# One transformer block on one NeuronCore: the down-projection's whole first pass by seven products, its sums turned back inside the second pass

## The chip, the cores and the metric

The kernel runs on one core of a Trainium2 chip. The metric is the device time of one execution in microseconds (us). The kernel before takes 1741.13 us, the median of three runs (1739.67 to 1741.83). The profiled execution, to which all rows of the trace belong, took 1740.01 us.

Five engines work in parallel, each on its own list of instructions in a fixed order: TensorE (PE in the profile, with its weight loads as PEld), VectorE (DVE), ScalarE (ACT), GpSimd (POOL) and SyncE (SP), which here issues nearly all DMA transfers. An instruction that waits for another engine holds up everything behind it on its own engine.

## The reference

One block works on 2048 tokens of width 512 in float32: attention and a gated feed-forward part, each behind a layer norm that is scaled and shifted by a conditioning vector.

```python
x = A_x                                        # (1, 2048, 512)
mod = (silu(c) @ w_mod).reshape(1, 6, 1, 512)  # sa, ca, ga, sb, cb, gb
h = layernorm(x) * (1 + ca) + sa
q = (h @ wq)                                   # 32 heads of 128; 8 heads of keys and values
p = softmax(q @ k.T * 128 ** -0.5)             # keys: the last 512 of the cache
x = x + ga * (p @ v) @ wo
h = layernorm(x) * (1 + cb) + sb
x = x + gb * ((gelu(h @ w_gate) * (h @ w_up)) @ w_down)   # 512 -> 1792 -> 512
```

## The kernel before

**Precision.** Every float32 operand of a product is split into a high half (float16) and a low half (what the high half leaves, again float16). A product is three matmuls, high by high, high by low and low by high, summed in PSUM (`mm3`, called at line 90 of the profile's numbering). The high halves are made by ScalarE as a copy, the low halves by a subtraction on VectorE or POOL. Weights are scaled so that they fit float16: the row norms are squared and summed on ScalarE (`sumsq`), summed across partitions by two-column matmuls (`sums`, tile `pst`) and turned into scales by small POOL and VectorE instructions (`f_spread`, `d_spread`).

**Seven products.** A product of two by two blocks is made of seven block products instead of eight (`PROD`, `CHAIN`, `ORDER`). This takes sums and differences of blocks beforehand (of weights on POOL during their preparation; of activations `t1` to `t4`) and adding up of the seven results.

**Stages.** Attention runs in 512 steps of about 2.6 us (`T` = 512), each with one score tile `ps`, its row maximum on VectorE, its exponential on ScalarE (line 993), its halves, a transpose by DMA (`pt<-p`, issued by SyncE) and the products with the values (`po`). The tokens go through in two halves of 1024. Projections of queries (`qa`, `qb`, `qc`) and of the attention's output (`py<-wo,ot`) fill TensorE between the score tiles. In the second half of attention the feed-forward weights are prepared beside this: loaded, scaled, combined on POOL, split, and stored to DRAM (`kept<-stage`). `prep_set` does so for the gate and up weights, `prep_wd` for the down weights. Their steps are planned by labels of attention steps (`sched`, `at`), and their buffers come from small pools: `raw` (five buffers, shared with the combination blocks `cb`, the staged products and later the rows `yr`), `rw` (two) and `wr` (two). A load is issued by SyncE when the buffer's earlier user has finished.

**Feed-forward part.** It starts at about 1345 us and has two passes of 1024 tokens. Each pass goes over seven pairs `n` of 128-wide tiles of the 1792 inner columns (`NP` = 7, so `n` = 0 to 13), and each pair has two projections `q = 2n + m`: gate (`m` = 0) and up (`m` = 1). Each projection is seven products of six matmuls in the order 1, 2, 6, 7, 5, 4, 3 (`ORDER`), in PSUM tiles `fa`, `fb`, `fc`. ScalarE copies the first, the second and the third chain's beginning out of PSUM (`keep`, line 887, tiles `fg`, `u`, `fu`), VectorE adds the rest (line 1272), and gate results go through GELU on ScalarE (line 1278); up results are multiplied with them on VectorE (line 1288), and the product is split (`high_of`, line 1298, and `low_of`, line 1302) for the down-projection.

**Down-projection.** In each pass the pairs up to the fifth (`turned(n)` true) use seven products. Their result comes transposed (columns of the model in partitions, tokens along the row), is scaled with a column per partition (`dyc`) and summed in float32 in SBUF over the pairs (`yt_add`, line 1678, tiles `yt`, VectorE). Sums of the activations' blocks for it are made on POOL (`sums_of`, line 1314). The last two pairs of each pass (`NROW` = 2) use plain row products (`y_tasks`, tile `py`), whose result has tokens in partitions and is added to the rows `acc` by VectorE (line 954). The plain weights carry the output's gain per column; the turned ones have it in `dyc`. So the transposed sums have to be turned back: ScalarE splits each float32 word into two 16-bit planes (`yt_turn`, line 1697, `yu<-yt`), a DMA transposes them (`yv<-yu`), POOL joins them again into rows (`yt_row`, line 1715, `yr<-yv`) and adds them to `acc` (`whole`, line 1657). In both passes this happens during the last two pairs: the chain ends with the fifth pair, and the sums turn while the row products run. The rows after attention (`y1`) are loaded to `acc` at the same place (`rows_in`).

**Order of the work.** The order on each engine is that in which the code issues it, with no planner behind it in this part. `tick` advances a counter after each product, and `put_off(d, f)` issues `f` that many products later. Products of the previous pair's down-projection are inserted between the products of the projection, after product index 1, 2, 5 and 6 (`y_next`), two at a time. Fetches of the next weights are issued at fixed product indices (`f_at(q, k, ...)`).

## Time and profile before

| what | value |
|---|---|
| median of three runs | 1741.13 us (1739.67 to 1741.83) |
| profiled execution | 1740.01 us |
| its span, first to last instruction | 1737.8 us |
| TensorE busy | 1712.5 us, 8020 matmuls |
| VectorE busy | 1426.1 us |
| ScalarE busy | 1242.4 us |
| POOL busy | 1056.9 us |
| moved by DMA | 339.82 MB, mean 196 GB/s |

How to read it: the page gives the busy time of each engine over the whole span, while the answers for a window (from:to in us from the start of the span) give it by stage. A row of the timeline has the start, the duration, the engine, the line of the kernel (L90 is line 90), the operation, the tile written and the tiles read, the shapes and a count of joined instructions; in brackets stands the time for which the engine had stood idle, and what ended it. A matmul's own duration is that of its passage through a pipeline: the next one starts before it ends, so the spacing of starts is what counts. A wait is put down to what came last. Rows of groups give busy time and mean duration in ns, then idle time before them.

### The profile page before, as it was taken

To read this page: it belongs to the slowest core of one execution; us is meant where nothing else is said; L and a number is where in the kernel's file an instruction comes from. 1 tells how busy PE (TensorE), PEld (TensorE's weight loads), DVE (VectorE), ACT (ScalarE), POOL (GpSimd) and SP (SyncE) were. 2 spreads that over 40 slices of the span, in tenths; PEclk is the share of its full clock that TensorE was granted. 3 is DMA by queue.
4 is the path that set the end of the run, shared out by engine and by line. 5 is a ranking of instruction groups with operands and counts; after the bars stand their busy time and mean duration, and the time that the engine had idled before them with its cause. 6 is when DMAs were issued, how large, how long until landed. Compare 5 with 4: busy or idle time off the path is not lost.

```text
span 1737.8 us, 26247 instructions
## 1 busy us (share of the span) xinstructions
PE 1712.5 (99%) x8020; PEld 786.6 (45%) x8022; DVE 1426.1 (82%) x2462; ACT 1242.4 (71%) x2797; POOL 1056.9 (61%) x1274
## 2 busy tenths in 40 slices
PE   7999999999999999999999999999999999999998
PEld 4444444444444444444444444444444444444444
DVE  7898898988888899888888888888986778666666
ACT  6988788888878777897778787777785455533442
POOL 4889778776788884654665665754720346733424
PEclk9999999999999999999999999999999999999999
DMA  7999999999999999999999999999996556633353
GB/s 233 222 202 213 216 212 208 222 203 221 219 216 233 201 209 187 213 209 229 199 221 223 207 230 210 198 229 214 199 189 151 158 160 207 167 121 119 95 157 103
DMA packets 690636, 339.82 MB, mean 196 GB/s; under 512 B 578880, under 2 KB 601408, under 8 KB 690496
## 3 DMA queue, kind: packets, MB, share of 16 engines
q1 hardware_dynamic: 690208, 337.63, 86.0%
q8 instruction: 63, 1.03, 0.3%
q14 instruction: 77, 0.63, 0.1%
q10 hardware_dynamic: 288, 0.52, 0.1%
HBM read 135.66 MB, written 61.87 MB: 114 GB/s over the span
## 4 chain that ended last, share of the span: by engine, by line
PE 86%; DVE 5%; ACT 4%; POOL 2%; DMA 2%; issue 1%; SPq 0%; DVEq 0%; POOLq 0%; ACTq 0%
PE py L90 20%; PE po L90 17%; PE ps L90 17%; PE qa L90 8%; PE fa L90 7%; PE qc L90 4%; PE fc L90 4%; PE ya L90 2%; PE qb L90 2%; PE fb L90 2%; DMA pt<-p 1%; PE yc L90 1%; ACT p L1005 1%; ACT ee L993 1%; PE pq L90 1%
## 5 line engine op out<-in xcount | busy, mean ns | idle before, releaser
L993 ACT ACTIVATE ee<-ps,nm 128x512 f32<-128x512 f32 x512 | 350.0, 684 | 191.9 <-DVE nm L984 189.8
L1010 DVE SCALAR_TENSOR_TENSOR p<-ee,rr,p 128x512 f16<-128x512 f32 x512 | 460.1, 899 | 4.7 <-ACT p L1005 4.3
L984 DVE TENSOR_REDUCE nm<-ps 128x1 f32<-128x512 f32 x512 | 350.1, 684 | 104.5 <-PE ps L90 101.1
L90 PE MATMUL ps<-k,qt 128*128 128x512 f16 x1536 | 414.9, 379 | 6.4 <-ACT ee L993 5.3
L1005 ACT ACTIVATE p<-ee,rr 128x512 f16<-128x512 f32 x512 | 364.5, 712 | 20.0 <-DVE rr L1001 10.1
L90 PE MATMUL po<-pt,v 128*128 128x512 f16 x1536 | 373.0, 379 | 2.0 <-DMA pt<-p 1.9
L90 PE MATMUL py<-wo,ot 128*128 128x512 f16 x1536 | 371.5, 379 | 0.0
L90 PEld LDWEIGHTS <-w 128*128 128x128 f16 x2184 | 213.3, 98 | 261.5 <-issue 4.2
L90 PEld LDWEIGHTS <-v 128*128 128x128 f16 x1536 | 149.8, 98 | 184.5 <-issue 2.4
L90 PEld LDWEIGHTS <-ot 128*128 128x128 f16 x1536 | 150.3, 98 | 181.6 <-DVE ot L742 0.5
L90 PEld LDWEIGHTS <-qt 128*128 128x128 f16 x1536 | 145.9, 98 | 177.7 <-issue 4.9
L1314 POOL TENSOR_TENSOR fg<-fg 128x512 f32<-128x512 f32 x40 | 52.8, 1319 | 153.9 <-DVE fg L1288 151.5
L742 DVE SCALAR_TENSOR_TENSOR ot<-po,ot 128x512 f16<-128x512 f32 x128 | 87.7, 685 | 39.3 <-ACT ot L741 38.9
L1298 ACT ACTIVATE at<-fg 128x512 f16<-128x512 f32 x86 | 53.9, 628 | 90.9 <-DVE fg L1288 75.4
L993 ACT ACTIVATION_READ_ACCUMULATOR ee<-ps,nm 128x1 f32 x512 | 99.9, 195 | 0.0
L954 DVE SCALAR_TENSOR_TENSOR acc<-py,ysc,acc 128x512 f32<-128x512 f32 x128 | 94.7, 739 | 5.3 <-PE py L90 5.3
L235 POOL TENSOR_TENSOR lw<-lw,half__86 128x1 f32<-128x1 f32 x37 | 23.4, 633 | 105.4 <-DVE lw L185 105.3
L90 PE MATMUL qa<-t,w 128*128 128x512 f16 x348 | 84.9, 379 | 0.0
L90 PE MATMUL fa<-t,w 128*128 128x512 f16 x336 | 81.6, 379 | 1.8 <-ACT fg L887 0.9
L397 POOL TENSOR_TENSOR rs<-rs,nhalf 128x1 f32<-128x1 f32 x32 | 18.8, 586 | 102.6 <-DVE rs L391 99.8
L741 ACT ACTIVATE ot<-po 128x512 f16<-128x512 f32 x128 | 73.8, 577 | 5.0 <-PE po L90 5.0
L159 POOL TENSOR_TENSOR stage<-rw,stage 128x512 f16<-128x512 f32 (+1 forms) x56 | 64.4, 1150 | 4.7
(241 smaller groups left out, 2761.5 us busy)
## 6 DMA issues: line engine op xcount, KB each, us to landing
w<-kept SPq DMA_DIRECT2D x123, 256.0 KB, 3.3
wo<-kept SPq DMA_DIRECT2D x70, 256.0 KB, 3.2
kept<-stage SPq DMA_DIRECT2D x61, 256.0 KB, 3.2
raw<-in_wo SPq DMA_DIRECT2D x56, 256.0 KB, 3.2
kept<-w SPq DMA_DIRECT2D x39, 256.0 KB, 3.2
rw<-in_wq SPq DMA_DIRECT2D x38, 256.0 KB, 3.2
hs<-hf SPq DMA_DIRECT2D x32, 256.0 KB, 2.8
pt<-p SPq DMA_TRANSPOSE x512, 3.5
```

The source lines that it names most:

```text
L90: nc.tensor.matmul(ps, a, b, start=first and n == 0, stop=last and n == 2, skip_group_check=chain)
L159: nc.gpsimd.tensor_tensor(dst[:, 1, :], src, dst[:, 0, :], op=ALU.subtract)
L235: nc.gpsimd.tensor_tensor(out, out, half_, op=ALU.pow)
L741: nc.scalar.activation(t[:, 0, :], src, AF.Copy, scale=scale)
L742: return lambda: nc.vector.scalar_tensor_tensor(t[:, 1, :], src, scale, t[:, 0, :], op0=ALU.mult, op1=ALU.subtract)
L954: nc.vector.scalar_tensor_tensor(acc[ti], st["p"], by, acc[ti], op0=ALU.mult, op1=ALU.add)
L984: nc.vector.tensor_reduce(nm, E[t]["ps"], axis=AX.X, op=ALU.max, negate=True)
L993: nc.scalar.activation(e, E[t]["ps"], AF.Exp, bias=E[t]["nm"], scale=1.0, accum_out=sm[:, t % 2:t % 2 + 1])
L1005: nc.scalar.activation(p16[:, 0, :], E[t]["e"], AF.Copy, scale=E[t]["r"])
L1010: nc.vector.scalar_tensor_tensor(p16[:, 1, :], E[t]["e"], E[t]["r"], p16[:, 0, :], op0=ALU.mult, op1=ALU.subtract)
L1298: nc.scalar.activation(t[:, 0, :], g, AF.Copy)
L1314: nc.gpsimd.tensor_tensor(g[o], g[a], g[b], op=ALU.subtract)
```

## The change

All seven pairs of the first pass now take the seven products in the down-projection (`turned(n)` is true for `n < NP`); in the second pass the last two pairs keep the row products. Since the two forms need differently prepared weights, the down weights of pairs 5 and 6 (counted from 0) are prepared twice: in turned form at the old place, stored under `wd`, and as plain rows at steps 455 and 490 of attention, stored under `wr` (`by_rows` gives their columns in `dsc` and `dysc`). The chain of the first pass thus ends with pair 6, whose products run during pair 7 of the second pass, and the sums of the first 1024 tokens are split, transposed and joined there. The joining copy `yr` of the first pass moves from POOL to ScalarE (`yt_row`); POOL then adds the row of `y1`, loaded into buffers of tag `h` (`rows_of_first`), to it, and the row goes out by DMA two products later (`first_out`). Splits and copies are put off by other numbers of products than before.

In the projections, the GELU of block 11 is put off by three products instead of two, the high half of block 11 of the very last up projection by two; the high halves of `t1`, `t2`, `t3`, `t4` are issued 2, 4, 4, 5 products later (before: 2, 4, 3, 5; for the first pair now 4, 5, 6, 6 and before 4, 6, 5, 6), and the low halves in the order `t2`, `t1`, `t3`, `t4` at 5, 5, 6, 6 (one more each for the first pair).

```diff
--- before.py
+++ after.py
@@ -172,7 +172,7 @@
 
     for name, n in (("kmax", HKV), ("kinv", HKV), ("vmax", HKV), ("vsc", HKV), ("wsc", HQ // 2), ("qsc", HQ // 2),
                     ("ksc", HQ // 2), ("osc", HKV), ("ysc", HKV), ("fsc", NF), ("finv", NF), ("gsc", NF // 2),
-                    ("dsc", NF // 2), ("dysc", NF // 2), ("dyc", KT * NF // 2), ("ma", 1), ("mf", 1), ("gam", 2)):
+                    ("dsc", NF // 2 + NROW), ("dysc", NF // 2 + NROW), ("dyc", KT * NF // 2), ("ma", 1), ("mf", 1), ("gam", 2)):
         stats(name, n)
 
     def col(name, i=0):
@@ -292,7 +292,11 @@
 
     def turned(n):
 
-        return n % NP < NP - NROW
+        return n < NP or n % NP < NP - NROW
+
+    def by_rows(n):
+
+        return NP + n % NP - (NP - NROW)
 
     def f_spread(i, m):
         w = little("lw", 1, 2)
@@ -304,18 +308,19 @@
             pool_ts(g, col("finv", i), 1.0 / GU)
             then(lambda: nc.vector.reciprocal(g, g))
 
-    def d_spread(n, m, more):
+    def d_spread(n, m, more, rows_):
         w, t = little("lw", 1, 2), little("lt", 1, 2)
         norm2(w, m, 2, 1.0)
-        pool_ts(w, w, 1.0 if turned(n) else col("gam", 1), 1.0 / TOP14)
+        d = by_rows(n) if rows_ else n
+        pool_ts(w, w, col("gam", 1) if rows_ else 1.0, 1.0 / TOP14)
         pool_ts(w, w, 1e-30, 1.0, ALU.max)
         pool_ts(t, col("finv", 2 * n), 2.0 ** 19, col("finv", 2 * n + 1))
-        pool_ts(col("dysc", n), t, 2.0 ** 19, w)
-        if turned(n):
+        pool_ts(col("dysc", d), t, 2.0 ** 19, w)
+        if not rows_:
             pool_ts(ST["dyc"][:, KT * n:KT * (n + 1)], cols[:, 5, :], col("dysc", n))
 
         def second():
-            nc.vector.reciprocal(col("dsc", n), w)
+            nc.vector.reciprocal(col("dsc", d), w)
             more()
 
         then(second)
@@ -1282,7 +1287,7 @@
 
         def result(key, src):
             if m == 0:
-                put_off(2 if key == "11" else 0, gelu(key, src)[0])
+                put_off(3 if key == "11" else 0, gelu(key, src)[0])
             else:
                 g = G[n, key]
                 nc.vector.scalar_tensor_tensor(g, g, col("gsc", n % NP), src, op0=ALU.mult, op1=ALU.mult)
@@ -1302,7 +1307,7 @@
             eng.tensor_tensor(t[:, 1, :], g, t[:, 0, :], op=ALU.subtract)
 
         def parts(key, g):
-            high_of(key, g)
+            put_off(2 if key == "11" and q == NQ - 1 else 0, lambda: high_of(key, g))
             if key in ("22", "21"):
                 st.setdefault("low", []).append(lambda: low_of(key, g, nc.vector))
             else:
@@ -1312,10 +1317,11 @@
             g = {k: G.pop((n, k)) for k in ("11", "12", "21", "22")}
             for o, a, b in (("11", "12", "11"), ("12", "22", "12"), ("22", "22", "11"), ("21", "21", "22")):
                 nc.gpsimd.tensor_tensor(g[o], g[a], g[b], op=ALU.subtract)
-            late = 0 if n else 2
-            for key, o, high, low in (("t1", "11", 2, 5), ("t3", "12", 3, 6), ("t2", "22", 4, 5), ("t4", "21", 5, 6)):
-                put_off(high + (late if high < 5 else late // 2), lambda key=key, o=o: high_of(key, g[o]))
-                put_off(low + late // 2, lambda key=key, o=o: low_of(key, g[o], nc.gpsimd))
+            src = {"t1": "11", "t2": "22", "t3": "12", "t4": "21"}
+            for key, high in zip(src, (2, 4, 4, 5) if n else (4, 5, 6, 6)):
+                put_off(high, lambda key=key: high_of(key, g[src[key]]))
+            for key, low in (("t2", 5), ("t1", 5), ("t3", 6), ("t4", 6)):
+                put_off(low + (not n), lambda key=key: low_of(key, g[src[key]], nc.gpsimd))
 
         def out_(key, src):
             if not hold:
@@ -1401,7 +1407,7 @@
         sched(b + 9, (outs[1][1], [lambda: made(1, RAW[key][0]), keep_it(1)]), b + 12)
         sched(b + 10, (outs[2][1], [lambda: made(2, RAW[key][1]), keep_it(2)]), b + 13)
 
-    def prep_wd(n, b):
+    def prep_wd(n, b, rows_=False):
         m, st = {}, {}
         outs = [staged() for _ in range(4)]
         l, r = slice(0, 256), slice(256, 512)
@@ -1416,12 +1422,12 @@
             sumsq(m["m"][:, k:k + 1], st[k])
 
         def more():
-            if not turned(n):
+            if rows_:
                 m["g"] = pool.tile([P, D], F32, tag="gs", name="gs", bufs=1)
-                pool_ts(m["g"], rows[5], col("dsc", n))
+                pool_ts(m["g"], rows[5], col("dsc", by_rows(n)))
 
         def spread():
-            d_spread(n, m["m"], more)
+            d_spread(n, m["m"], more, rows_)
 
         def make(k):
             nc.gpsimd.tensor_tensor(st[k], st[k], m["g"], op=ALU.mult)
@@ -1431,7 +1437,7 @@
             return outs[k][0]["t"] if k < 3 else outs[k][0]["t"][:, :, l]
 
         def keep_it(k):
-            return lambda: store(("wd", n, k), out(k), 0)
+            return lambda: store(("wr" if rows_ else "wd", n, k), out(k), 0)
 
         def tt(o, a, c, op):
             nc.gpsimd.tensor_tensor(o, a, c, op=op)
@@ -1451,7 +1457,7 @@
             tt(st[0][:, l], st[1][:, r], st[0][:, l], ALU.subtract)
             tt(st[1][:, l], st[1][:, l], st[0][:, l], ALU.subtract)
 
-        if not turned(n):
+        if rows_:
             sched(b, (lambda: load(0), [lambda: stat(0), nop]), b + 7, kind="wr")
             sched(b + 1, (lambda: load(1), [lambda: stat(1), spread, nop]), b + 4, b + 9, kind="wr")
             for k in range(2):
@@ -1470,9 +1476,11 @@
         prep_set(2 * n, b)
         prep_set(2 * n + 1, b + 13)
         prep_wd(n, b + 21)
+    for n, b in ((NP - 2, T - 57), (NP - 1, T - 22)):
+        prep_wd(n, b, True)
     def wd_fetch(n, k):
         t = get_wo()
-        WO["f", n, k] = fetch(("wd", n % NP, k), t if k < 3 else t[:, :, 0:256])
+        WO["f", n, k] = fetch(("wd" if turned(n) else "wr", n % NP, k), t if k < 3 else t[:, :, 0:256])
 
     for k, pos in zip((0, 3, 2, 1), (T - 1, T + 1, T + 3, T + 6)):
         at(pos, lambda k=k: wd_fetch(0, k))
@@ -1686,8 +1694,15 @@
             load_acc(ti, y1[ti], None, *tags[i // 2])
             back.add(ti)
 
-    for g in range(2):
-        f_at(2 * (NP * g + NP - NROW) - 1, 6, lambda g=g: rows_in(g, 0, (("rw", NRW), ("wr", NWR))))
+    def rows_of_first():
+        for j in range(QT):
+            t = pool.tile([P, 2, D], F32, tag="h", name="yo", bufs=NB)
+            for k in range(2):
+                acc[2 * j + k] = t[:, k, :]
+                dma(acc[2 * j + k], y1[2 * j + k])
+
+    f_at(2 * NP + 1, 3, rows_of_first)
+    f_at(2 * (2 * NP - NROW) - 1, 6, lambda: rows_in(1, 0, (("rw", NRW), ("wr", NWR))))
 
     def yt_turn(g, c, qb):
 
@@ -1704,19 +1719,28 @@
         split()
         put_off(3, turn)
         YR["n"] = YR.get("n", 0) + 1
-        if YR["n"] % (2 * QT) == QT:
+        if YR["n"] == 3 * QT:
             put_off(4, lambda: rows_in(g, 1, (("acc", 2 * QT),) * 2))
 
     def yt_row(g, qb, i):
         t = YR["t", qb].rearrange("p c (h i) q -> p c q h i", h=2)
         ti = 2 * QT * g + QT * qb + i
-        assert ti in back
         r = raw("yr")
-        nc.gpsimd.tensor_copy(r.bitcast(U16).rearrange("p (c q h) -> p c q h", c=KT, h=2), t[:, :, :, :, i])
-        joined[ti] = r
-        whole(ti)
+        to = r.bitcast(U16).rearrange("p (c q h) -> p c q h", c=KT, h=2)
+        if g:
+            assert ti in back
+            nc.gpsimd.tensor_copy(to, t[:, :, :, :, i])
+            joined[ti] = r
+            whole(ti)
+        else:
+            nc.scalar.activation(to, t[:, :, :, :, i], AF.Copy)
+            put_off((1, 1, 3, 3)[i] if qb == 0 else 1, lambda: first_out(ti, r))
         if i == QT - 1:
             del YR["t", qb]
+
+    def first_out(ti, r):
+        nc.gpsimd.tensor_tensor(r, r, acc[ti], op=ALU.add)
+        put_off(2, lambda: dma(rows_of(out, ti), r))
 
     ADDS = {1: ((0, 0),), 2: ((0, 0),), 6: ((0, 1),), 5: ((1, 1),), 7: ((1, 1),), 4: ((1, 0),), 3: ((0, 1),)}
     YORDER = ((1, 2, 6, 5, 7, 3, 4), (1, 2, 6, 7, 5, 4, 3))
@@ -1739,13 +1763,14 @@
             def post(k, p=p, st=st):
                 (i, qb), = ADDS[k]
                 yt_add(n, 2 * i + p, qb, st[CHAIN[k][0]])
-                if n % NP == NP - NROW - 1 and k in LAST:
+                if n in (NP - 1, 2 * NP - NROW - 1) and k in LAST:
                     i, qb = LAST[k]
                     c, g = 2 * i + p, n // NP
-                    put_off(2 if k == 3 else 1, lambda: yt_turn(g, c, qb))
+                    put_off((2 if g else 4 if p else 3) if k == 3 else 1, lambda: yt_turn(g, c, qb))
                     if p and k in (3, 4):
                         for r in range(QT):
-                            put_off((7 if k == 4 else 8) + r // 2, lambda r=r: yt_row(g, qb, r))
+                            d = (7 if k == 4 else 8) + r // 2 if g else 6 + r // 2 if k == 4 else 10 + r
+                            put_off(d, lambda r=r: yt_row(g, qb, r))
 
             tasks += [(lambda k=k, f=group: f(k), lambda k=k, f=post: f(k)) for k in YORDER[p]]
         return [tasks[k:k + 2] for k in range(0, len(tasks), 2)]
@@ -1770,7 +1795,7 @@
             for qi, (a, b) in enumerate((("11", "21"), ("12", "22"))):
                 for i in range(QT):
                     nexty.append(y_tasks((2 * (n // NP) + qi) * QT + i, [lambda n=n, a=a: A[n, a], lambda n=n, b=b: A[n, b]],
-                                         [("f", n, 0), ("f", n, 1)], col("dysc", n % NP), f_final))
+                                         [("f", n, 0), ("f", n, 1)], col("dysc", by_rows(n)), f_final))
     while nexty:
         y_next()
         tick()
```

## The prediction

> **What bounds the kernel now.** I read the page's busy line first, then the table of windows, then the waits of TensorE, and last the timeline at single places.
>
> ```profile
> span 1737.8 us, 26247 instructions
> PE 1712.5 (99%) x8020; PEld 786.6 (45%) x8022; DVE 1426.1 (82%) x2462; ACT 1242.4 (71%) x2797; POOL 1056.9 (61%) x1274
> ```
>
> TensorE is busy 1712.5 of 1737.8 us. So a change is worth the matmuls it removes, plus the waits of TensorE it removes or makes. The windows (us from:to, length, busy time and count of PE, PEld, DVE, ACT, POOL, then clock, DMA share, GB/s) show by stage what else is near its limit.
>
> ```profile
> 300.00:600.00 300.00, 299.23 (x1416) 137.28 (x1415) 263.07 (x473) 250.84 (x611) 238.68 (x306) 1.00 1.01 218
> 1250.00:1260.00 10.00, 10.00 (x48) 4.57 (x47) 9.41 (x15) 8.48 (x20) 5.17 (x5) 1.00 1.02 225
> 1260.00:1290.00 30.00, 30.00 (x141) 13.62 (x140) 26.03 (x42) 24.73 (x58) 11.28 (x9) 1.00 1.06 216
> 1300.00:1310.00 10.00, 10.00 (x48) 4.47 (x46) 7.99 (x15) 7.13 (x17) 0.00 (x0) 1.00 0.70 144
> 1345.00:1440.00 95.00, 94.30 (x436) 42.50 (x435) 73.64 (x114) 45.13 (x74) 36.62 (x42) 1.00 0.57 163
> 1440.00:1500.00 60.00, 58.19 (x268) 26.09 (x267) 44.38 (x61) 35.02 (x57) 47.93 (x38) 1.00 0.62 182
> 1500.00:1600.00 100.00, 100.00 (x465) 45.27 (x463) 61.62 (x86) 37.48 (x60) 40.13 (x32) 1.00 0.47 137
> ```
>
> In attention (to about 1340 us) the DMA engines are full (share about 1) and ScalarE and VectorE are at 80 to 90%, yet TensorE misses nearly nothing. In the feed-forward part there is air on every other engine, and TensorE loses only 0.7 us in 95 and 1.8 in 60. A full stretch gives the price of a matmul: 100.00 / 465 = 0.215 us. The clock is 1.00 throughout. The waits of TensorE in 1300:1460 (first two rows), 1460:1600 (three) and 1600:1738 (last) name what is lost (total, times, longest):
>
> ```profile
> PE fa L90 <- ACT fg L887: 0.6, 2, 0.3
> PE ya L90 <- POOL at L1302: 0.3, 1, 0.3
> ...
> PE ya L90 <- DVE yt L1678: 0.7, 1, 0.7
> PE fa L90 <- ACT u L887: 0.5, 1, 0.5
> PE fa L90 <- ACT fg L887: 0.3, 1, 0.3
> ...
> PE fa L90 <- ACT u L887: 0.4, 1, 0.4
> ```
>
> These rows leave out the refilling of the pipeline. The two waits of pair 5's up projection show how much:
>
> ```profile
> 1490.64 0.38 PE L90 MATMUL yb<-at,wo 128*128 128x512 f16 x1
> 1491.70 0.81 PE L90 MATMUL ya<-at,wo 128*128 128x512 f16 x3 [0.68 <-DVE yt L1678]
> 1492.99 0.81 PE L90 MATMUL fa<-t,w 128*128 128x512 f16 x3 [0.48 <-ACT u L887]
> ...
> 1491.42 1.04 ACT L1697 ACTIVATE yu<-yt 128x1024 uint16<-128x1024 uint16 x1
> 1492.37 0.57 ACT L887 ACTIVATE u<-fa 128x512 f32<-128x512 f32 x1
> ...
> 1488.61 1.72 DVE L1288 SCALAR_TENSOR_TENSOR fg<-fg,gsc,fu 128x512 f32<-128x512 f32 x1
> ...
> 1487.16 2.62 POOL L576 TENSOR_TENSOR cb<-cb 128x512 f32<-128x512 f32 x2
> ```
>
> Start to start, 1490.64 + 0.215 against 1491.70 is 0.85 lost, and 1491.70 + 3 x 0.215 against 1492.99 is 0.64: the wait in the brackets plus 0.17. The second has a plain cause: the copy of the sum out of PSUM (L887) stands on ScalarE behind a split of the turned sums (L1697, 1.04 us).
>
> **The change, part by part.**
> *Matmuls.* Pairs 5 and 6 of the first pass now take 2 x 7 products of three matmuls each (84 of 512 columns) where 8 row sums took 96 (py). 12 x 0.215 = **-2.6**. Four statistics matmuls of 2 columns more: +0.1 at most. Beside this row, the Trainium skill, "TensorE: Matmul & The Clock Gate", section "Back-to-back issue gap", gives a sustained spacing of about 131 ns for 512 columns; by it the 12 would be worth an estimated 1.6, and the sum 1.0 less good. The stretch of 465 matmuls at 0.215 decides against it here.
>
> *GELU and high halves put behind ScalarE's copies.* The copy fg (L887) that TensorE awaits was behind the GELU or the high halves (L1298) that now come later. Three first-pass waits: 0.6 + 0.3 + 3 x 0.17 = 1.4, of which I leave 0.1 for a new queue of two copies: -1.3. The POOL wait of pair 0's sums, 0.3 + 0.17: -0.5, since the lows are now issued in the order t2, t1, t3, t4. The last up projection's wait, 0.4 + 0.17: -0.6. In the second pass four gaps of this kind are too short for a wait row:
>
> ```profile
> 1589.47 0.81 PE L90 MATMUL yb<-at,wo 128*128 128x512 f16 x3
> 1590.23 1.02 PE L90 MATMUL fa<-t,w 128*128 128x512 f16 x4
> ```
>
> 1590.23 - 1589.47 - 0.645 = 0.115, four times: -0.4. Sum **-2.8**. If the later high halves make the next up projection's products wait, half of it comes back; each operand still has over one product (1.3 us) to spare, so I take nothing for it, and if that cover is gone each costs 0.3 to 0.5 like those removed.
>
> *Pair 5's up projection.* The splits leave this place (they now follow pair 6): the 0.64 goes. The 0.85 hangs on VectorE: L1288 took 1.72 there against a mean of 0.895 and pushed yt back.
>
> ```profile
> L1288 DVE SCALAR_TENSOR_TENSOR fg<-fg,gsc,fu 128x512 f32<-128x512 f32 x13 | 11.6, 895 | 0.5
> L1302 POOL TENSOR_TENSOR at<-fg,at 128x512 f16<-128x512 f32 x40 | 46.0, 1182 | 0.9 <-ACT at L1298 0.9
> L1314 POOL TENSOR_TENSOR fg<-fg 128x512 f32<-128x512 f32 x40 | 52.8, 1319 | 153.9 <-DVE fg L1288 151.5
> L1697 ACT ACTIVATE yu<-yt 128x1024 uint16<-128x1024 uint16 x16 | 16.5, 1045 | 0.0
> L1715 POOL COPY yr<-yv 128x1024 uint16<-128x1024 uint16 x16 | 19.9, 1264 | 34.3 <-DMA yv<-yu 34.3
> ```
>
> POOL was in two subtractions (L576) meanwhile, and they stay. I count half of the 0.85: **-1.1** in all. The Trainium skill, "GPSIMD Engine Reference", section "Specifications", says that GpSimd shares its SBUF interfaces with VectorE, with contention where a VectorE instruction has two inputs in SBUF. The 1.72 against 0.895 agrees; by this rule the whole 0.85 stays, and POOL's 16 added sums and lows spread more of it.
>
> *Work that stays beside TensorE.* POOL gets 8 more sums (1.32) and 8 lows (1.18) in the first pass, 20 us where 36.62 of 95 and 47.93 of 60 are busy; VectorE gets 28 chain steps for 16 row sums, about 9 us at 0.75. Both have room; nothing. The first half's rows go out from a new sum on POOL, with yr as before, far ahead of the end; the last pass and the tail don't change.
>
> *The turning back at pair 7.* The splits, then eight row copies, now on ScalarE, lie in pair 8's gate and up projection (q16, q17). The nearest row is L1697, same shape and engine, 1.045; POOL's 1.264 is the other bound. Laid along the products of this projection (six matmuls, 1.29 us each), two of these copies stand ahead of the copy s1 that TensorE awaits: at 1.045 it is an estimated 0.2 to 0.4 early, at 1.264 up to 0.45 late, and at 1.6 1.9 late over both products concerned. One split before u2 costs 0.1. I take **+0.25** (0 to 2).
>
> *Preparing the weights twice.* Pairs 5 and 6 are now stored in turned form (four products) and as plain rows: 12 more transfers of 256 KB or 128 KB, 2.88 MB, in 1170 to 1300 us, and their work on POOL, VectorE and ScalarE. Three places:
> First, ScalarE squares the reloaded rows, and stands until they have landed:
>
> ```profile
> wr<-in_wd SPq DMA_DIRECT2D x14, 256.0 KB, 3.3
> ```
>
> The plan gives these loads about one or two steps of attention (2.6 us each) after POOL frees their buffer, the landing takes 3.3: up to 1.8 us of standing, I estimate, at two steps. The spare time of ScalarE's exponential is 1.65 in the place shown next, so little of it reaches TensorE. **+0.3** (0 to 1.5).
> Second, the end of pair 6's preparation meets the last combination blocks, which share its five raw buffers:
>
> ```profile
> 1245.15 0.53 SPq L96 DMA_DIRECT2D kept<-stage  x1
> 1249.65 0.32 SPq L96 DMA_DIRECT2D cb<-hs  x1
> 1251.39 0.56 SPq L96 DMA_DIRECT2D kept<-stage  x1
> ...
> 1252.96 1.27 POOL L576 TENSOR_TENSOR cb<-cb 128x512 f32<-128x512 f32 x1 [0.99 <-DMA cb<-hs]
> ...
> 1253.41 0.62 ACT L374 ACTIVATE t<-cb 128x512 f16<-128x512 f32 x1
> 1253.93 0.68 ACT L993 ACTIVATE ee<-ps,nm 128x512 f32<-128x512 f32 x1
> ...
> 1256.26 0.81 PE L90 MATMUL ps<-k,qt 128*128 128x512 f16 x3
> ```
>
> The load cb waits on SyncE for the store's landing (4.5 us). In the new order one more store follows, and POOL must make the third product, which waits for that store's buffer, before its subtraction L576: about 0.6 to 1.2 of standing and 1.2 of work, so L576 ends near 1255.6 to 1257.9 instead of 1254.2. ScalarE's copy L374 waits for it in a fixed order, and behind L374 stands the exponential L993 on which scores wait: ScalarE is 2.2 to 4.5 late, where L993's end (1254.6) has 1.65 before the scores at 1256.26. **+1.6** (0 to 3): the middle.
> Third, the full DMA engines:
>
> ```profile
> 1252.06 1.29 SPq L1014 DMA_TRANSPOSE pt<-p  x1
> ...
> 1258.20 0.81 PE L90 MATMUL po<-pt,v 128*128 128x512 f16 x3
> ...
> pt<-p SPq DMA_TRANSPOSE x512, 3.5
> ```
>
> A transpose issued at 1252.06 is used at 1258.20; with the median landing of 3.5, 2.6 us are spare. Bulk transfers can slip into the emptier stretch from 1300 us. **+0.25** (0 to 10).
>
> Sum: -2.6 + 0.1 - 2.8 - 1.1 + 0.25 + 0.3 + 1.6 + 0.25 = **-4.0**. The profiled execution took 1740.01 (span 1737.8, 2.2 around it), 1.1 under the median of 1741.13. Against its own time this is 1736.0, against the median **1737.1**.
>
> **The rivals.**
> *Stalls only move.* ScalarE's order is fixed, so a high half put off can make the next product wait instead; then only the matmuls and the 0.64 count: -2.6 - 0.6 + 2.5 = -0.7, 1740.4. For it: every high half still has to be made. Against: ScalarE is busy 45.13 of 95 there.
> *The preparation hides altogether.* The store lands early, POOL's wait and ScalarE's with it: -6.5 without the costs, 1734.6. For it: the windows around 300 to 600 us with the same work run at 299.23 of 300. Against: the 4.5 us landing is in the trace.
> *Slower: the DMA engines decide.* 2.88 MB at the 216 GB/s of a share of 1.06 are 13.3 us of DMA time; if transposes wait behind them, their 2.6 us of slack are used up and TensorE ends about 10 us late, 1741.1 - 6.1 + 10 = 1745. It decides from the point where the transposes land over 6 us after issue for several units. For it: 1.02 to 1.06 from 1250 to 1290 us. Against: 300 to 600 us at 1.01 without loss.
> *The turned form buys nothing.* The row copies on ScalarE take 1.6 and yr comes late: +1.9 instead of 0.25, 1738.8; part of the middle cases below.
>
> **How the numbers follow.** Chances: forecast 0.42, stalls move 0.22, all hidden 0.16, DMA or a longer wait at the end of attention 0.15, row copies 0.05. The measurement tells about 0.2% from no change, 3.5 us: 1737.6 to 1744.6. Forecast's better 0.30 and all hidden give faster 0.46; the forecast's other 0.12, the moved stalls and the row copies give the same, with 0.01 of the DMA case, 0.40; the rest, 0.14, slower. The range: 1733.5, below "all hidden" with VectorE's other 0.4 us too, up to 1744.5, just under the DMA case; 0.14 + 0.04 lie outside. The forecast's own range is 1735 to 1739.5.
>
> **What would show it.** Right: py falls by 96 and ya, yb, yc rise by 84; the waits of fa on L887 fall below 0.5 in the feed-forward part; no split (L1697) ahead of u in pair 5; L993 late behind L374 once between 1250 and 1260, with a TensorE gap of 1 to 3 us. Wrong: windows of 1180 to 1300 with PE more than 3 us below full, pt landings above 6 us, or new waits of fa on L1298's neighbours, yr copies above 1.3 us.

## The result and the profile after

The changed kernel takes 1734.95 us (median of six runs, 1734.13 to 1737.56) against 1740.74 us of six runs of the kernel before: a ratio of 0.9969, 95% interval 0.9958 to 0.9979, or 5.8 us less (3.7 to 7.3). The forecast was 4.0 less, 1737.1. Its profiled execution took 1736.03 us, 3.98 less than that of before (1740.01); it lies 1.1 above the median of its kernel, and that of before 0.7 below its own.

The page of the changed kernel, the lines on the span and the busy times:

```profile
span 1734.2 us, 26336 instructions
PE 1710.5 (99%) x8012; PEld 786.3 (45%) x8012; DVE 1430.4 (82%) x2476; ACT 1254.9 (72%) x2819; POOL 1093.9 (63%) x1328
```

POOL has 37 us more to do, TensorE 2.0 less. The groups of TensorE in the feed-forward part (all matmuls have one tile shape; busy time, mean ns, idle before):

```profile
L90 PE MATMUL ya<-at,wo 128*128 128x512 f16 x288 | 76.0, 379 | 0.9 <-DVE yt L1686 0.7
L90 PE MATMUL yc<-at,wo 128*128 128x512 f16 x144 | 39.1, 379 | 0.3 <-POOL at L1307 0.3
L90 PE MATMUL py<-wo,at 128*128 128x512 f16 x96 | 21.9, 379 | 0.0
L90 PE MATMUL yb<-at,wo 128*128 128x512 f16 x72 | 19.5, 379 | 0.0
```

There were 192 py before and 420 in the other three together (240, 120, 60); now it is 96 and 504. So 12 matmuls of 0.215 us are gone, as worked out. (Line numbers have moved: L374 is now L379, L576 L581, L887 L892, L993 L998, L1288 L1293, L1302 L1307, L1314 L1319, L1678 L1686, L1697 L1712. L1736 is the row copy, L1742 the new addition `yr + yo`.)

The windows of the feed-forward part (the same columns and stretches as before), and all waits of TensorE in it:

```profile
1345.00:1440.00 95.00, 95.00 (x441) 43.03 (x440) 75.29 (x117) 44.89 (x75) 37.07 (x42) 1.00 0.58 165
1440.00:1500.00 60.00, 59.25 (x276) 26.69 (x274) 45.83 (x63) 29.96 (x52) 47.73 (x38) 1.00 0.48 149
1500.00:1600.00 100.00, 99.08 (x456) 44.44 (x455) 68.08 (x97) 54.15 (x80) 48.26 (x40) 1.00 0.55 166
...
PE ya L90 <- DVE yt L1686: 0.7, 1, 0.7
PE fa L90 <- ACT fg L892: 0.5, 1, 0.5
PE yc L90 <- POOL at L1307: 0.3, 1, 0.3
```

The first stretch is now full, and no wait is left there. In the second the wait of ya on yt stays, 0.7. In the third, full before, 0.9 is missing: there are new waits. Start to start (each spacing of two matmuls less 0.215 us, so with the refilling and with gaps too short for a wait row), TensorE lost 4.7 us in the feed-forward part before and loses 2.9 now. With the matmuls this is 2.6 + 1.8 = 4.4 less. Counted from the gate projection of pair 1 to the end of the span, the two traces differ by 4.1; the changed run came to that place 0.5 us later, and it was already 0.7 late at 104 us, where both kernels do the same work.

The new waits follow one another. The timeline of the changed kernel, VectorE and then POOL, during the up projection of pair 8 (start, duration):

```profile
1573.55 1.43 DVE L1307 TENSOR_TENSOR at<-fg,at 128x512 f16<-128x512 f32 x1
1576.26 1.46 DVE L1293 SCALAR_TENSOR_TENSOR fg<-fg,gsc,u 128x512 f32<-128x512 f32 x1
1579.82 2.13 DVE L1307 TENSOR_TENSOR at<-fg,at 128x512 f16<-128x512 f32 x2
...
1573.16 1.27 POOL L1742 TENSOR_TENSOR yr<-yr,yo 128x512 f32<-128x512 f32 x1 [3.05 <-ACT yr L1736]
1575.91 1.27 POOL L1742 TENSOR_TENSOR yr<-yr,yo 128x512 f32<-128x512 f32 x1 [1.48 <-ACT yr L1736]
1579.53 1.27 POOL L1742 TENSOR_TENSOR yr<-yr,yo 128x512 f32<-128x512 f32 x1 [2.35 <-ACT yr L1736]
1583.41 5.33 POOL L1319 TENSOR_TENSOR fg<-fg 128x512 f32<-128x512 f32 x4 [2.61 <-DVE fg L1293]
```

In each of these three rows VectorE starts while POOL is in an addition, and ends 0.5 to 0.6 us behind the end of that addition (1573.16 + 1.27 = 1574.43, and 1573.55 + 1.43 = 1574.98; the third row joins two instructions, of which the first is held up). These instructions read two tiles in SBUF. Those that read PSUM keep their 0.75 us. VectorE falls behind, POOL's sums (L1319) start late, then the high halves on ScalarE (L1303), and the copy fg (L892) that TensorE awaits stands behind these. ScalarE and TensorE there:

```profile
1587.42 1.15 ACT L1303 ACTIVATE at<-fg 128x512 f16<-128x512 f32 x2 [1.59 <-POOL fg L1319]
1588.48 0.58 ACT L892 ACTIVATE fg<-fa 128x512 f32<-128x512 f32 x1
...
1589.11 1.46 PE L90 MATMUL fa<-t,x 128*128 128x512 f16 x6 [0.47 <-ACT fg L892]
```

### The profile page after: what moved, and what is told of

Same layout as the page of the kernel before. It is cut to its first block, busy times and chain, and to the rows that moved or that the text cites. A ratio compares the mean times of both kernels' runs of the same rounds, so it can differ in the third digit from the quotient of the medians.

```text
span 1734.2 us, 26336 instructions
## 1 busy us (share of the span) xinstructions
PE 1710.5 (99%) x8012; PEld 786.3 (45%) x8012; DVE 1430.4 (82%) x2476; ACT 1254.9 (72%) x2819; POOL 1093.9 (63%) x1328
## 4 chain that ended last, share of the span: by engine, by line
PE 88%; DVE 4%; ACT 4%; DMA 2%; POOL 1%; issue 1%; SPq 0%; DVEq 0%; POOLq 0%; ACTq 0%
PE py L90 18%; PE po L90 17%; PE ps L90 17%; PE fa L90 8%; PE qa L90 8%; PE fc L90 4%; PE qc L90 4%; PE ya L90 3%; PE fb L90 2%; PE qb L90 2%; PE yc L90 2%; DMA pt<-p 1%; ACT ee L998 1%; ACT p L1010 1%; DVE nm L989 1%; PE pq L90 1%
## 5 line engine op out<-in xcount | busy, mean ns | idle before, releaser
L998 ACT ACTIVATE ee<-ps,nm 128x512 f32<-128x512 f32 x512 | 349.7, 683 | 186.1 <-DVE nm L989 181.0
L1319 POOL TENSOR_TENSOR fg<-fg 128x512 f32<-128x512 f32 x48 | 62.9, 1310 | 148.5 <-DVE fg L1293 145.6
L1303 ACT ACTIVATE at<-fg 128x512 f16<-128x512 f32 x92 | 56.4, 626 | 83.7 <-DVE fg L1293 63.6
L998 ACT ACTIVATION_READ_ACCUMULATOR ee<-ps,nm 128x1 f32 x512 | 99.9, 195 | 0.0
L90 PEld LDWEIGHTS <-wo 128*128 128x128 f16 x504 | 49.3, 98 | 61.0 <-issue 2.0
L90 PE MATMUL ya<-at,wo 128*128 128x512 f16 x288 | 76.0, 379 | 0.9 <-DVE yt L1686 0.7
```

The lines of the kernel that those rows point to most:

```text
L90: nc.tensor.matmul(ps, a, b, start=first and n == 0, stop=last and n == 2, skip_group_check=chain)
L998: nc.scalar.activation(e, E[t]["ps"], AF.Exp, bias=E[t]["nm"], scale=1.0, accum_out=sm[:, t % 2:t % 2 + 1])
L1303: nc.scalar.activation(t[:, 0, :], g, AF.Copy)
L1319: nc.gpsimd.tensor_tensor(g[o], g[a], g[b], op=ALU.subtract)
```

## The experiments

Each kernel was timed beside the kernel before, on the same chip in the same set of runs: 1740.42 us for `order_only`, `old_order`, `prep_only` and `no_add`, 1740.81 for `add_late`, `cb_shift`, `late_shift` and `add_dve`, 1740.49 for `late_four` and `copy_pool`. "Lost" is what TensorE loses in the feed-forward part, start to start, in the profiled execution; a spacing of twice 0.215 without a wait, where the trace lacks a record, is not counted.

| kernel | us | ratio to before, 95% interval | lost, us |
|---|---|---|---|
| before | 1740.74 | | 4.7 |
| changed | 1734.95 | 0.9969 (0.9958 to 0.9979) | 2.9 |
| order_only | 1736.38 | 0.9976 (0.9967 to 0.9985) | 1.1 |
| old_order | 1741.39 | 1.0006 (0.9998 to 1.0015) | 8.6 |
| prep_only | 1740.41 | 1.0000 (0.9991 to 1.0009) | 4.8 |
| no_add | 1732.98 | 0.9956 (0.9944 to 0.9969) | 1.2 |
| add_late | 1733.31 | 0.9962 (0.9948 to 0.9975) | 0.8 |
| cb_shift | 1734.25 | 0.9966 (0.9954 to 0.9979) | 2.0 |
| late_shift | 1733.14 | 0.9963 (0.9951 to 0.9976) | 0.8 |
| add_dve | 1735.76 | 0.9973 (0.9963 to 0.9983) | 1.6 |
| late_four | 1732.91 | 0.9959 (0.9946 to 0.9973) | 0.3 |
| copy_pool | 1736.21 | 0.9975 (0.9966 to 0.9984) | 2.9 |

### The new order alone, and the change without it

`order_only` is the kernel before with these edits and no others; `old_order` is the changed kernel with them undone.

```diff
-                put_off(2 if key == "11" else 0, gelu(key, src)[0])
+                put_off(3 if key == "11" else 0, gelu(key, src)[0])
...
-            high_of(key, g)
+            put_off(2 if key == "11" and q == NQ - 1 else 0, lambda: high_of(key, g))
...
-            for key, o, high, low in (("t1", "11", 2, 5), ("t3", "12", 3, 6), ("t2", "22", 4, 5), ("t4", "21", 5, 6)):
...
+            for key, high in zip(src, (2, 4, 4, 5) if n else (4, 5, 6, 6)):
...
+            for key, low in (("t2", 5), ("t1", 5), ("t3", 6), ("t4", 6)):
```

> The kernel before with nothing but the new distances of GELUs, high and low halves. Theory A (ScalarE's order made these waits): the waits of fa on L887 and of ya on POOL in the feed-forward part go, all but the two of pair 5's up projection (0.85 and 0.64): 0.50 + 0.44 + 0.25 + 0.49 + 0.48 + 4 x 0.11 + 0.60 = 3.2 us less, about 1737.5 against 1740.7. Rival B (stalls only move): new waits on L1298 or L1302 of the same sum, 1740 to 1741.

> The changed kernel with the old distances of GELUs, high and low halves, so the seven products, the double preparation and the turning back alone. Theory A (parts add up): 3.2 us over the changed kernel, about 1738.2, with the waits of fa on ACT back at seven places and more in pairs 5 and 6, which are now turned too. Rival B: 1735, the same as the changed kernel. If the turning back wants the new distances, more than 4 us over it.

The waits of TensorE in the feed-forward part, first of `order_only`, then of `old_order`:

```profile
PE fa L90 <- ACT u L887: 0.4, 1, 0.4
PE fa L90 <- ACT fg L887: 0.2, 1, 0.2
```

```profile
PE fa L90 <- ACT fg L892: 3.3, 6, 1.3
PE ya L90 <- DVE yt L1685: 1.4, 2, 0.7
PE ya L90 <- POOL at L1307: 0.9, 2, 0.5
PE fa L90 <- ACT u L892: 0.4, 1, 0.4
```

`order_only` measured 4.0 us less than before (2.6 to 5.7), where 3.2 was expected, and 3.6 less is lost in its trace. Of these 3.6, 0.85 is the wait of ya in pair 5's up projection, which the order was not meant to remove; it hangs on a race, and with the new order it is there in two traces of six (see the section on that projection). Without it the order is worth 2.8. The other waits went, and one small one came: fg, 0.2 (0.34 with the refilling), at 1502 us behind a split of the turned sums. The remaining 0.4 behind u is the splits of pair 5, as expected. `old_order` measured 6.4 us more than the changed kernel: not the 3.2 of parts that add up, but the third case of the expectation, over 4. Against before it is 1.0 more, with an interval (0.3 less to 2.6 more) that includes no difference. Its 12 matmuls fewer are paid for by new waits. Pair 5 now has POOL's sums and late high halves too (0.76 lost start to start at 1507 us), and the late sums of pair 8 meet the old order with a wait of 1.3 and one of 0.5 (2.15 lost at 1590 to 1596). Another 0.85, at 1464 us, is of the kind that a race decides in pair 5's up projection. The parts do not add up: without the new order the seven products gain nothing that these runs show; on top of it they save 1.4 by the medians (1736.38 to 1734.95), though the runs of the two kernels overlap.

### The double preparation alone

`prep_only` is the kernel before, with pairs 5 and 6 prepared twice; the turned form is stored and never read.

```diff
+    for n, b in ((NP - 2, T - 57), (NP - 1, T - 22)):
+        prep_wd(n, b, True)
...
-        WO["f", n, k] = fetch(("wd", n % NP, k), t if k < 3 else t[:, :, 0:256])
+        WO["f", n, k] = fetch(("wd" if turned(n) else "wr", n % NP, k), t if k < 3 else t[:, :, 0:256])
```

> The kernel before with the double preparation of the down weights of pairs 5 and 6 and nothing else (the turned form is stored and never read). By the prediction's terms 0.3 + 1.6 + 0.25 = 2.15 us slower (0 to 14 by their ends), with TensorE waiting between 1179 and 1262 us. By the trace of the changed kernel, which shows no gap of TensorE there: no difference, 1740 to 1741.5.

It measured 1740.41 against 1740.42, with the interval at 1.6 us on either side. The waits of TensorE from 1170 to 1300 us in `prep_only`:

```profile
PE ps L90 <- ACT ee L998: 0.5, 2, 0.3
```

The changed kernel has no row in this stretch. But the chain that the prediction described is there. POOL and ScalarE of the changed kernel at the end of attention, and the score they lead to:

```profile
1251.77 0.62 POOL L158 TENSOR_SCALAR stage<-wr 128x512 f16<-128x512 f32 x1 [3.02 <-DMA kept<-stage]
1253.90 2.94 POOL L581 TENSOR_TENSOR cb<-cb 128x512 f32<-128x512 f32 x2
...
1255.20 0.63 ACT L379 ACTIVATE t<-cb 128x512 f16<-128x512 f32 x1 [1.20 <-POOL cb L581]
1255.73 0.67 ACT L998 ACTIVATE ee<-ps,nm 128x512 f32<-128x512 f32 x1
...
1256.75 0.81 PE L90 MATMUL ps<-k,qt 128*128 128x512 f16 x3
```

POOL stood 3.02 us for the landing of a store, then made the product and the subtractions. The copy L379 stood 1.20 us for POOL, and the exponential behind it (1253.93 before) starts at 1255.73. It ends at 1256.40, and TensorE goes on at 1256.75 without a gap. ScalarE was 1.3 late after the 0.5 that this run was late anyway, not 2.2 to 4.5, and the 1.65 to spare covered it. In `prep_only` the same place cost one of the two waits of up to 0.3. The DMA engines, at a share of 1.0 to 1.1 as before, took the added transfers without a late transpose: from 1180 to 1300 us the transposes `pt<-p` landed 3.7 us after their issue at the median and 5.1 at most, where it was 3.6 and 7.0 before.

### POOL's additions left out, put late, or given to VectorE

`no_add` leaves the rows after attention out of the first half's result:

```diff
     def first_out(ti, r):
-        nc.gpsimd.tensor_tensor(r, r, acc[ti], op=ALU.add)
```

> The changed kernel without POOL's addition of the rows after attention to the first half's rows (first_out's sum is left out; the rows go out without it). Theory A (POOL's additions slow VectorE's instructions with two inputs in SBUF, L1307 and L1293, to 1.4 us from 0.7, and the sums of pair 8 come 1.6 late): these take 0.7 to 0.75 at 1573 to 1580 us, POOL's sums start near 1581.8, and the waits of 1572 to 1592 us (1.7 in all) go: 1733.3. Rival C (ScalarE's row copies L1736 delay the high halves): the waits stay, 1735.

`no_add` measured 2.0 us less than the changed kernel, 1732.98, where 1.7 was expected, and all its runs lie below all those of the changed kernel. Its row copies are where they were. Its timeline at the places shown above, 0.8 us earlier here, VectorE and POOL:

```profile
1572.70 0.68 DVE L1307 TENSOR_TENSOR at<-fg,at 128x512 f16<-128x512 f32 x1
1575.42 0.75 DVE L1293 SCALAR_TENSOR_TENSOR fg<-fg,gsc,u 128x512 f32<-128x512 f32 x1
1578.26 1.28 DVE L1307 TENSOR_TENSOR at<-fg,at 128x512 f16<-128x512 f32 x2
...
1581.07 5.33 POOL L1319 TENSOR_TENSOR fg<-fg 128x512 f32<-128x512 f32 x4 [17.47 <-DVE fg L1293]
```

0.68 in place of 1.43, 0.75 in place of 1.46, 1.28 in place of 2.13. The waits from 1580 to 1600 are gone; one gap of 0.08 is left in this up projection. The row copies on ScalarE, still there, are not their cause. Of the 1.2 that it still loses, 0.9 is the wait in pair 5.

`add_late` keeps the sum, and issues the additions of rows 3 to 7 behind POOL's low halves of pair 9's gate projection:

```diff
-            put_off((1, 1, 3, 3)[i] if qb == 0 else 1, lambda: first_out(ti, r))
+            if qb == 0 and i < 3:
+                put_off((1, 1, 3)[i], lambda: first_out(ti, r))
+            else:
+                f_at(18, 6, lambda: first_out(ti, r))
```

> The changed kernel with five of POOL's eight additions (rows 3 to 7) issued behind POOL's low halves of pair 9's gate projection, where VectorE has no instruction with two inputs in SBUF for some 6 us. Theory L (such an instruction and a POOL instruction run one after the other): the additions cost nothing there, L1307 and L1293 take 0.7 at 1573 to 1580 us, 1733 to 1733.5, as without them. Rival W (POOL's additional work costs as such, wherever it stands): about 1735, or the waits appear in the next up projection.

It measured 1733.31, as expected, and leaves nothing out. (In `f_at(18, 6, ...)` 18 is q = 2n + m, the gate projection of pair 9; pairs are counted from 0.) Its POOL at that place:

```profile
1584.99 4.51 POOL L1307 TENSOR_TENSOR at<-fg,at 128x512 f16<-128x512 f32 x4
1589.45 6.20 POOL L1745 TENSOR_TENSOR yr<-yr,yo 128x512 f32<-128x512 f32 x5
```

The five additions cost nothing where VectorE reads PSUM, except for the last, which reaches the next up projection and meets L1293 there (1.43 from 1594.77): the next wait is at 1597.57, 0.4 of ya on yt.

`add_dve` has `nc.vector` for `nc.gpsimd` in `first_out`.

> The changed kernel with the eight additions on VectorE in place of POOL. Theory L (only the overlap of the two engines costs): each costs VectorE 0.68 with nothing in its way, against 0.7 lost per collision before; in the up projection VectorE is nearly full, so five additions there make the sums 2 to 3 us late: as the changed kernel or up to 1.5 us slower, 1735 to 1736.5. Rival W (POOL's work costs as such): 1733 to 1734, as without the additions.

1735.76: within the expected span, and 2.8 more than without the additions. The 0.8 over the changed kernel is not clear of the noise; the 2.5 over `add_late`, in the same set of runs, is. Without a collision, each addition takes VectorE 0.68, and five of them in a projection where it is nearly full made TensorE wait 0.94 for yt:

```profile
1579.70 0.81 PE L90 MATMUL ya<-at,wo 128*128 128x512 f16 x3 [0.94 <-DVE yt L1689]
```

So both exist, the collision and the plain work; POOL is the better place if it is at the right time.

### Pair 5's up projection

```diff
-    for p, (q, at_) in enumerate(((59, (61, 62, 62, 63, 64, 65, 66, 67, 68)), (70, (75, 76, 76, 77, 78, 79, 80, 81, 82)))):
+    for p, (q, at_) in enumerate(((59, (61, 62, 62, 63, 64, 65, 66, 67, 68)), (70, (75, 77, 77, 77, 78, 79, 80, 81, 82)))):
```

> The changed kernel with one high half of the combination blocks (L379) moved behind the copy fu on ScalarE, so that POOL's subtractions L581 come about 1.5 us later in pair 5's up projection. Theory L: L1293 at about 1487.1 no longer starts just behind a POOL instruction of 1.3 us, it takes 0.75 to 1.3 in place of 1.78, and the wait of ya on yt (0.91 with its refill) falls below 0.5: 0.5 to 0.9 us less than the changed kernel, about 1734.3. Rival S (the wait is VectorE's load of instructions as such): it stays, 1735; POOL's sums of pair 5 late by over 1 us would show as new waits of 0.5 or more between 1498 and 1512.

1734.25, 0.7 less, as expected, though the runs of the two kernels overlap, so that the time alone does not show it. In its trace the wait went altogether, and the others stayed (2.0 lost). Three fences for one place: VectorE's L1293 (L1288) and POOL's subtractions beside it, in the changed kernel, in `order_only`, and in `cb_shift`:

```profile
1487.10 1.78 DVE L1293 SCALAR_TENSOR_TENSOR fg<-fg,gsc,fu 128x512 f32<-128x512 f32 x1
...
1485.73 2.61 POOL L581 TENSOR_TENSOR cb<-cb 128x512 f32<-128x512 f32 x2
```

```profile
1486.95 0.75 DVE L1288 SCALAR_TENSOR_TENSOR fg<-fg,gsc,fu 128x512 f32<-128x512 f32 x1
...
1485.70 3.13 POOL L576 TENSOR_TENSOR cb<-cb 128x512 f32<-128x512 f32 x2
```

```profile
1486.27 0.81 DVE L1293 SCALAR_TENSOR_TENSOR fg<-fg,gsc,fu 128x512 f32<-128x512 f32 x1
...
1486.61 1.60 POOL L581 TENSOR_TENSOR cb<-cb 128x512 f32<-128x512 f32 x1
```

In the first two kernels POOL's second subtraction starts at about 1487.1. In the first VectorE comes just behind it and takes 1.78; in the second VectorE comes 0.1 us ahead, takes 0.75, and it is POOL's pair that takes 3.13 in place of 2.61. Whoever starts first goes through, and the other waits. Nine of the kernels have the same order on POOL at this place. In the profiled executions of five (before, changed, `old_order`, `prep_only`, `no_add`) VectorE came 0.03 to 0.11 us behind POOL's subtraction, took 1.71 to 1.78, and the wait was there. In those of four (`order_only`, `add_late`, `add_dve`, `copy_pool`) it came 0.10 to 0.12 ahead, took 0.75, and there was no wait. At so small a distance it is a race. The three kernels with the old order all lost it, the six with the new order lost it twice; whether the order shifts the odds, one profile of each kernel can't tell. In the three kernels with the shift (`cb_shift`, `late_shift`, `late_four`) VectorE took 0.81, and none has the wait.

### Both, and what is best

`late_shift` is `add_late` and `cb_shift` together. `late_four` is the same with only the four rows of the second block added late (row 3 stays).

> Both of the two before. If they add up: 2 + 0.6 less than the changed kernel, about 1732.3 to 1732.7. If POOL's later work in pair 5 costs what the wait gained: as with the late additions alone, 1733 to 1733.5.

> As late_shift, but only the four rows of the second row copy's block are added late (row 3 as in the changed kernel). Four additions take 5 us in place of 6.2 and end before VectorE's next L1293, so the wait of 0.5 at the beginning of pair 9's up projection (1597 to 1599) goes: 1732.5. If row 3 at its old place collides instead, a new wait of up to 0.5 at 1570 us and the same time as late_shift, 1733.

1733.14 and 1732.91: the two do not add up to 2.3 less than the changed kernel by the median (1.8 and 2.0), and between them these runs do not tell. By the traces the shift had nothing to add to `add_late`, whose profiled execution lacked pair 5's wait anyway: both lose 0.8. In the profiled execution of `late_four` only 0.3 us is lost in the feed-forward part; the wait at pair 9's up projection went, as expected. By its median `late_four` is the fastest of the complete kernels, 7.6 us under before.

### The row copies on POOL

```diff
-            nc.scalar.activation(to, t[:, :, :, :, i], AF.Copy)
+            nc.gpsimd.tensor_copy(to, t[:, :, :, :, i])
```

> The changed kernel with the first half's row copies back on POOL, which adds the rows as before. If every POOL instruction excludes VectorE's instructions with two inputs in SBUF, the copies (1.26 each, one input) do so as well: L1307 and L1293 of 1.4 us and more at more places in the up projection, 1 to 2 us over the changed kernel, 1736 to 1737. If only POOL instructions with two inputs do, the copies cost nothing by themselves and ScalarE is freer: 1734 to 1735.

1736.21, 1.3 over the changed kernel, in the first theory's span; the runs of the two overlap. Its trace loses 2.9 as the changed kernel's does, but without pair 5's 0.9, so pairs 8 and 9 lose 0.9 more. VectorE and POOL of `copy_pool` at one place:

```profile
1574.70 1.17 DVE L1293 SCALAR_TENSOR_TENSOR fg<-fg,gsc,u 128x512 f32<-128x512 f32 x1
...
1574.17 1.15 POOL L1736 COPY yr<-yv 128x1024 uint16<-128x1024 uint16 x1
```

The copy has one input, and VectorE ends 0.55 behind it as behind an addition. So here it is not POOL's second input that counts, and this is no single case: in the twelve traces 26 such VectorE instructions met a copy `yr<-yv` on POOL, and all ended 0.54 to 0.55 behind it. The loss is not this alone: POOL's own queue is longer too, and its sums start later for it; the run does not separate the two.

## Why the prediction was right, and where its steps failed

*Matmuls, -2.6:* right; 12 fewer in the groups, at the same 0.215. `late_four`, with hardly a wait left, lies 3.5 us under `order_only`: 0.8 is its smaller loss, and 2.6 are the matmuls. The sustained 131 ns per matmul that the prediction cited from the Trainium skill, "TensorE: Matmul & The Clock Gate", section "Back-to-back issue gap", would leave an estimated 1.6 for them; the traces have 0.215 us throughout.

*GELU and high halves, -2.8:* right, in size too. Alone they measured -4.0 (2.6 to 5.7); the traces have 3.6, and 2.8 without the 0.85 of pair 5 that the race decides. The rival that the stalls only move is out. What the prediction did not see is that the seven products need this order: without it the change is 6.4 slower, and nothing of its gain is left.

*Pair 5's up projection, -1.1:* the splits' 0.64 went; of the 0.85, half was counted, and in the profiled execution all of it stayed (0.91). The cause is the one that the prediction named, VectorE's L1288 beside POOL's L576: the traces have the wait whenever VectorE came second, and never when it came first. It is a race of 0.1 us, lost in two of the six traces with the new order, so "half" was a fair guess without its reason.

*Work that stays beside TensorE, 0:* this step failed. "Both have room" was read from busy times, and room did not help: POOL's additions hold up VectorE's instructions with two inputs in SBUF. `no_add` puts the cost at 2.0 us by the medians, 1.7 by the traces. The rule that the prediction cited from the Trainium skill, "GPSIMD Engine Reference", section "Specifications", says so, and the trace agrees with 1.43 against 0.68; the prediction applied it to pair 5 and to POOL's sums and lows, and not to the additions, which it named ("a new sum on POOL") and priced at nothing.

*The turning back, +0.25:* the size was right for what it priced. A row copy on ScalarE takes 1.16, between the two bounds, and with the additions left out 0.08 is lost in its up projection. The 1.8 us of waits that follow belong to the step before.

*The double preparation, +2.15:* too much. Its term at the raw buffers, 1.6, was the mis-sized one: a wait of the kind described came, ScalarE was 1.3 late and not 2.2 to 4.5, and that fits into the 1.65 to spare. The working was off in two places. The 0.6 to 1.2 of standing and 1.2 of work that it names bring the end of L576 from 1254.2 to between 1256.0 and 1256.6, not between 1255.6 and 1257.9. And the copy at 1253.41 did not wait for that subtraction, which ended only at 1254.23; it waited for one that had ended by 1249.0 before, and that ends at 1255.2 in the changed kernel. `prep_only` gives 0.0, with 1.6 either way. With it the rival in which the DMA engines decide is out, and the rival in which the preparation hides altogether is right about the preparation. Its 1734.6 also lies nearer to the median of 1734.95 than the forecast's 1737.1 does, but it leaves out POOL's additions. Of the signs named, the exponential came late behind the copy as said, and the gap of 1 to 3 us on TensorE did not come.

So 2.15 too much at the preparation and 1.7 to 2.0 too little at POOL's additions nearly cancel, and the total came near for a reason that the steps don't share. That is luck, and so is the agreement of -4.0 with the -3.98 of two single profiled executions. The medians differ by 5.8, whose interval (3.7 to 7.3) holds both. Where the 5.8 exceeds the 4.4 of the traces, the cause is not shown; a race that falls otherwise from run to run is worth up to 0.9 of it.

## What to carry to other kernels

Room on two engines by their busy times is not room for both at once: look at which VectorE instructions read two tiles in SBUF, and put POOL's work where VectorE reads PSUM. A change that removes matmuls and an order that removes waits may only pay together, so price the order alone and the change alone before adding them. A wait that depends on a distance of 0.1 us between two engines is not a property of the kernel; move one of the two by a microsecond rather than count on it.

## What the runs showed of the hardware

In the feed-forward part of all twelve traces, VectorE's instructions that read two tiles of 128x512 in SBUF and POOL's instructions went one after the other wherever they met. 237 of VectorE's began behind a POOL instruction that had more than 0.25 us to go: each ended 0.54 to 0.55 us behind the end of that instruction, and took 0.81 to 1.80 us in place of 0.68 to 0.75. It made no difference whether POOL's had two inputs or one. The other way round, 79 of POOL's two-input instructions of 1.27 us began behind such a VectorE instruction: each ended 1.12 to 1.14 us behind its end, and took 1.55 to 1.79. Whichever came second waited, and the first kept its own time. VectorE's instructions that read one tile in PSUM and at most one in SBUF took at most 0.75 us in the 1503 cases in which they began beside a running POOL instruction.
